# Attention placed from slot 0, masks behind ReLUs, values in one slot: a windowed attention interleaved with an MLP

## The chip, the cores and the metric

The kernel runs on one core of a Trainium2 chip. The metric is device time in microseconds (us) of one execution. A ratio is the mean time of one kernel's fast runs over that of the other's of the same rounds, so it is not quite the ratio of the medians that are quoted. Engines are called as in the profile: PE is the tensor engine (PEld its weight loads), DVE the vector engine, ACT the scalar engine, POOL the GpSimd engine, SP the sync engine, which here only issues DMAs.

## The reference, cut to what matters

```python
# q, k, v: (8 batches, 8 heads, 576, 64) float32
scores = scale * np.matmul(q, k.transpose(0, 1, 3, 2))
mask = (rel >= 0) & (rel < 64)                 # causal, window of 64
attn = softmax(np.where(mask, scores, -1e9))
x = np.matmul(attn, v)                         # reshaped to (8, 576, 512)
h = (x.transpose(0, 2, 1) @ U @ V)             # low rank: U (576, 32), V (32, 576)
u = x + h.transpose(0, 2, 1)
out = u + np.maximum(u @ w_ch1, 0) @ w_ch2     # 512 -> 2048 -> 512
```

## The kernel before

The 8 x 576 rows make 9 chunks of 512 rows for the MLP. While the MLP of chunk c runs, the attention of batch b = c + 1 is woven into it. A chunk has 32 slots: slots 0 to 15 each compute one 128-row piece of the first product (four 512-column matmuls into a PSUM tile `psA`, then a ReLU that empties it, on DVE or ACT), slots 16 to 31 compute four row tiles of the second product, four quarters each, into `psU`. Work of the attention is appended to a slot and is issued behind that slot's MLP matmuls. In the traces DVE takes up its work in the order of issue; what that costs, waits of 0.22 to 0.49 us for ACT, is seen below.

Scores (`SC`) go to PSUM, ACT takes the exponential, and DVE multiplies by the mask at once:

```python
# in SC(j), one pair of heads; SC8 does the last block of all heads
nc.scalar.activation(out=dst, in_=sc[:], func=ACT.Exp, scale=scale)
if not spare:
    nc.vector.tensor_tensor(out=dst, in0=dst, in1=maskA..., op=ALU.mult)
```

The values of one row tile (`PV(t)`) are small matmuls into a PSUM tile of 2 x 512 float32 (`xr`), followed by a reciprocal and a multiplication on DVE. The low-rank product (`UM`) has 5 row tiles and 4 column groups of 32 in the array; the fifth tile reuses group 0:

```python
for t in ts:                                   # t = 0 .. 4
    g = t % 4
    nc.tensor.matmul(hh["ps"][g * R : (g + 1) * R, :], ub[odd][:, t, :],
                     x[:, t, :, :].rearrange("p h d -> p (h d)"),
                     start=(t < 4), stop=(t > 0))
```

The placement of the attention in the slots of a steady chunk, and of batch 1 in chunk 0:

```python
DVE_RELU = (1, 2, 3, 5, 6, 7, 9, 11)           # these ReLUs on DVE, the others on ACT
PLACE = {"S": [1, 1, 1, 4, 4], "PV": [9, 9, 12, 12, 12],
         "TX": [8, 9, 10, 11, 12], "U": [15], "V": [17, 18, 19],
         "UT": [18, 18, 19, 19, 20]}
PLACE_1 = {"T": [9, 9, 10, 10, 11, 11, 12, 12], "S": [10, 11, 12, 13, 13],
           "PV": [15, 15, 16, 17, 18], "U": [20], "V": [21, 22, 23],
           "UT": [23, 24, 25, 26, 27], "TX": [20, 22, 24, 26, 28]}
...
if b > 1:                                      # value rows shifted by half a tile, on DVE
    slots[8 if b == 2 else 0].append(lambda: shift_v(b, nc.vector.tensor_copy, range(NFULL)))
```

`T` transposes keys and queries of batch 1 on PE; `TX` does so for the next batch by DMA (SP issues ten DMA transposes per batch); `UT` turns the finished rows `un` into the next MLP input `uTc`, by DMA from batch 3 on. The second weight `w2b` is loaded in four pieces early in chunk 0, between the loads of batches 1 and 2.

The softmax here doesn't subtract the row's maximum and nothing guards it: scores larger than these inputs give would overflow.

Of the kernel before, what the change touches and what calls it, by code (L numbers as in the profile page):

```python
# [9 lines left out]
ALU = mybir.AluOpType  # L10

BF16 = mybir.dt.bfloat16
FP32 = mybir.dt.float32
# [3 lines left out]
def kernel(  # L17
# [11 lines left out]
    nc = tc.nc  # L29
    B, H, S, D = q.shape  # L30
    DM = H * D
    R = moe_U.shape[1]
    F = moe_w_ch1.shape[1]
    P = nc.NUM_PARTITIONS
    W = 64
# [202 lines left out]
    def attention(b, spare=False):  # L238
# [96 lines left out]
        def SC(j):  # L335
            def f():
# [10 lines left out]
                if not spare:  # L347
                    nc.vector.tensor_tensor(  # L348
                        out=dst, in0=dst, in1=maskA.rearrange("p g n w -> p g (n w)"), op=ALU.mult
                    )  # L350
            return f

        def SC8():
# [18 lines left out]
            dst = ptl[:]  # L372
            if not spare:
                mk = maskA[:, :, 2:3, :].rearrange("p g n w -> p n g w").to_broadcast([P, HP, 2, W])
                nc.vector.tensor_tensor(out=dst, in0=dst, in1=mk, op=ALU.mult)

        def PV(t):
            def f():
# [4 lines left out]
                packed = b >= NXU and len(blks) == 1  # L383
                if packed:
                    one = ps_tp.tile([P, CH], FP32, name="one", tag="tp")
                else:
                    xr = ps_big.tile([P, 2, CH], FP32, name="xr", tag="big")
                for h in range(H):
                    for blk in blks:
                        r0 = ((blk + odd) % 2) * W  # L390
                        if blk == 0:
                            rhs = va[:, 0, h, :]
                        elif blk % 2 == 1:
                            rhs = va[:, blk // 2, h, :]
                        else:
                            rhs = vb[:, blk // 2 - 1, h, :]
                        cols = slice((h % 4) * VW, (h % 4 + 1) * VW)
                        if packed:
                            dst = one[(h // 4) * W : (h // 4 + 1) * W, cols]
                        else:  # L400
                            dst = xr[r0 : r0 + W, h // 4, cols]
                        nc.tensor.matmul(  # L402
                            dst,
                            pts[:, h // 2, h % 2, blk, :] if blk < NB - 1 else ptl[:, h // 2, h % 2, :],
                            rhs,
                            start=True,
                            stop=True,
                        )
                if packed:
                    xv = one[:, 0 : 4 * VW].rearrange("p (h e) -> p h e", e=VW)  # L410
                    rcp = wk_pool.tile([P, 2, 4, 1], FP32, name="rcp", tag="rcp")
                    nc.vector.reciprocal(out=rcp[:, 0], in_=xv[:, :, D:VW])
                    for a in range(2):
                        rs = slice(a * W, (a + 1) * W)
                        nc.vector.tensor_tensor(
                            out=x[lo:hi, t, 4 * a : 4 * a + 4, :],
                            in0=xv[rs, :, 0:D],
                            in1=rcp[rs, 0].to_broadcast([W, 4, D]),
                            op=ALU.mult,
                        )  # L420
                    return
# [9 lines left out]
            return f  # L431

# [3 lines left out]
        def UM(ts):  # L436
            def f():
# [5 lines left out]
                for t in ts:  # L443
                    g = t % 4
                    nc.tensor.matmul(  # L445
                        hh["ps"][g * R : (g + 1) * R, :],
                        ub[odd][:, t, :],
                        x[:, t, :, :].rearrange("p h d -> p (h d)"),
                        start=(t < 4),
                        stop=(t > 0),  # L450
                    )
# [112 lines left out]
        tiles = list(range(NT))  # L564
        if odd and b >= NXU:
            tiles = tiles[1:] + tiles[:1]
        pcs["PV"] = [PV(t) for t in tiles]
# [17 lines left out]
    DVE_RELU = (1, 2, 3, 5, 6, 7, 9, 11)  # L585

    DVE_RELU_0 = (8, 9, 11, 13, 15)

    def mlp(c):
# [3 lines left out]
        def ch1(i):  # L593
            def f():
# [10 lines left out]
                if i in (DVE_RELU if c > 0 else DVE_RELU_0):  # L605
                    nc.vector.tensor_relu(out=c1[i][:], in_=ps[:])  # L606
                else:
                    nc.scalar.activation(out=c1[i][:], in_=ps[:], func=ACT.Relu)  # L608
# [29 lines left out]
        "S": [1, 1, 1, 4, 4],  # L638
        "PV": [9, 9, 12, 12, 12],
        "TX": [8, 9, 10, 11, 12],  # L640
        "U": [15],
        "V": [17, 18, 19],
        "UT": [18, 18, 19, 19, 20],
# [3 lines left out]
        "T": [9, 9, 10, 10, 11, 11, 12, 12],  # L647
        "S": [10, 11, 12, 13, 13],
        "PV": [15, 15, 16, 17, 18],
        "U": [20],  # L650
        "V": [21, 22, 23],
        "UT": [23, 24, 25, 26, 27],
# [3 lines left out]
        "S": [8, 8, 11, 11, 13],  # L656
        "PV": [16, 16, 18, 18, 20],
        "TX": [12, 13, 14, 15, 16],
# [69 lines left out]
    for c in range(NCH):  # L728
# [10 lines left out]
        if b < B:  # L739
# [14 lines left out]
            if b > 1:  # L754
                slots[8 if b == 2 else 0].append(lambda: shift_v(b, nc.vector.tensor_copy, range(NFULL)))
            place(b, ("S", "PV"), where)
# [37 lines left out]
```

## Time and profile before

| | before |
|---|---|
| median of the runs | 327.12 us (326.85 to 327.33, 4 runs) |
| profiled span | 325.1 us |
| PE busy | 309.4 us, 95% |
| steady chunk (starts of the first `psA` matmuls) | 33.28 us |
| a chunk of the MLP alone (the last whole one) | 27.63 us |

The page of the kernel before: busy time, the busy tenths of PE and of the DMA engines in 40 equal slices, and the costliest group of instructions (name of the tile written and read, shapes, count, busy us, mean ns of one, idle us of the engine before it and what ended that idle time).

```profile
PE 309.4 (95%) x2806; PEld 149.9 (46%) x2831; DVE 169.7 (52%) x311; ACT 96.8 (30%) x152; POOL 104.1 (32%) x134
...
PE   7789899999999999899999999999999999999995
...
DMA  7999999999999999999999993355300330020011
...
L597 PE MATMUL psA<-uTc,w1b 128*128 128x512 bf16 x576 | 131.9, 379 | 4.6 <-DVE c L606 2.9
```

PE is what bounds the kernel (95% busy), but until slice 24 (about 195 us) the DMA engines are 90% or more busy as well, all but the first slice. The idle time before `psA` is small in sum, and it sits in a few places. In the order of time of PE, chunk 5 of the kernel before (start, duration, line, operation, count, and in brackets the idle time just before and what ended it):

```profile
204.79 0.47 PE L326 MATMUL sc<-qf,kf 64*64 64x128 bf16 x23
205.45 2.75 PE L597 MATMUL psA<-uTc,w1b 128*128 128x512 bf16 x12 [0.18 <-DVE c L606]
208.58 1.89 PE L597 MATMUL psA<-uTc,w1b 128*128 128x512 bf16 x8 [0.39 <-DVE c L606]
...
211.04 2.76 PE L597 MATMUL psA<-uTc,w1b 128*128 128x512 bf16 x12
```

The first line shows only the part of its group that reaches into the window asked for. And DVE at the same time:

```profile
203.18 0.69 DVE L348 TENSOR_TENSOR pts<-pts,maskA 128x1024 bf16<-128x1024 bf16 x1 [0.49 <-ACT pts L346]
204.10 0.69 DVE L348 TENSOR_TENSOR pts<-pts,maskA 128x1024 bf16<-128x1024 bf16 x1 [0.23 <-ACT pts L346]
204.71 1.28 DVE L606 TENSOR_SCALAR c<-psA 128x512 bf16<-128x512 f32 x2
206.32 0.69 DVE L348 TENSOR_TENSOR pts<-pts,maskA 128x1024 bf16<-128x1024 bf16 x1 [0.33 <-ACT pts L346]
207.24 0.69 DVE L348 TENSOR_TENSOR pts<-pts,maskA 128x1024 bf16<-128x1024 bf16 x1 [0.22 <-ACT pts L346]
207.84 1.88 DVE L606 TENSOR_SCALAR c<-psA 128x512 bf16<-128x512 f32 x3
```

DVE stands at a mask until ACT has finished the exponential, while ReLUs whose inputs are complete or about to be queue up behind it (runs of two from 204.71 and of three from 207.84). There are only three PSUM buffers for `psA`, so PE waits for the ReLU. The bracket counts idle time after the modelled end of a matmul; from start to start the loss is larger, because matmuls overlap: 512-column matmuls of a steady stream start 216 ns apart, and the two gaps here are 0.25 and 0.55 us longer than they would otherwise be.

The low-rank product in the kernel before, in the order of time of PE:

```profile
183.95 0.61 PE L445 MATMUL pshh<-xs,ub 128*32 128x512 bf16 x5
184.49 1.68 PE L619 MATMUL psU<-w2b,c 128*128 128x512 bf16 x6
```

Four of the five start 4 ns apart; the fifth, on group 0 again, starts 216 ns after them. And the places where PE waits for DMA in chunks 0 and 2:

```profile
35.06 0.45 PE L262 MATMUL tpw<-ident,qg 96*64 96x96 bf16 x12 [1.27 <-DMA qg<-in_q_dram]
...
46.95 1.04 PE L619 MATMUL psU<-w2b,c 128*128 128x512 bf16 x4
48.30 1.04 PE L619 MATMUL psU<-w2b,c 128*128 128x512 bf16 x4
...
132.82 1.47 PE L597 MATMUL psA<-uTc,w1b 128*128 128x512 bf16 x6 [1.26 <-DMA uTc<-un]
```

The `psU` matmuls at 46.95 and 48.30 us use the second and third piece of `w2b`, and do not wait: the value matmuls of batch 1 stand between them.

Some matmul records are missing from a trace: now and then two `psU` matmuls seem to start 432 ns apart, which is twice 216. Such gaps are not counted as waits here.

### The profile page before, as it was taken

What the parts mean: (1) busy time and instruction counts of PE and PEld (TensorE: products, weight loads), DVE (VectorE), ACT (ScalarE), POOL (GpSimd) and SP (SyncE); (2) the same over time, 40 slices, a digit from 0 to 9 for tenths busy, and PEclk for the clock granted to TensorE, in tenths of its full rate; (3) what the DMA queues carried; (4) which work ended last, traced back from release to release, by engine and by line L of the source; (5) the groups of instructions that cost most, each with busy time, mean ns of one, the idle gap of its engine ahead of it and who ended that gap; (6) DMA issues with size and microseconds to landing.
All of it is one profiled execution on the core that took longest, in us unless ns stands there. A gap on an engine that the chain in (4) does not pass through costs nothing.

```text
span 325.1 us, 6773 instructions
## 1 busy us (share of the span) xinstructions
PE 309.4 (95%) x2806; PEld 149.9 (46%) x2831; DVE 169.7 (52%) x311; ACT 96.8 (30%) x152; POOL 104.1 (32%) x134
## 2 busy tenths in 40 slices
PE   7789899999999999899999999999999999999995
PEld 6544454544454444344444444444444444444442
DVE  4364686265557752585458554855476525115211
ACT  3636541327026220343033402440154002201400
POOL 8692697545545744475430500000000000000000
PEclk9999999999999999999999999999999999999999
DMA  7999999999999999999999993355300330020011
GB/s 112 164 224 195 162 193 160 118 188 176 129 147 227 128 141 142 225 144 149 134 204 185 103 175 105 65 95 93 109 2 3 87 115 8 2 97 32 2 65 65
DMA packets 151871, 39.56 MB, mean 122 GB/s; under 512 B 140960, under 2 KB 146080, under 8 KB 151840
## 3 DMA queue, kind: packets, MB, share of 16 engines
q0 software_dynamic: 100096, 18.36, 82.4%
q1 hardware_dynamic: 51744, 20.77, 36.5%
q8 instruction: 22, 0.36, 0.5%
q14 instruction: 9, 0.07, 0.1%
HBM read 37.14 MB, written 9.44 MB: 143 GB/s over the span
## 4 chain that ended last, share of the span: by engine, by line
PE 73%; DMA 12%; DVE 4%; ACT 4%; POOL 2%; SPq 2%; issue 1%; POOLq 0%; ACTq 0%
PE psU L619 33%; PE psA L597 30%; DMA qg<-in_q_dram 5%; ACT pts L346 3%; PE xr L402 3%; DMA vA<-in_v_dram 3%; DMA uTc<-un 3%; PE sc L326 2%; DMA qf<-qn 2%; PE psv L519 2%; SPq L285 1%; DVE pts L348 1%; PE pshh L445 1%; DVE c L606 1%; DVE un L532 1%
## 5 line engine op out<-in xcount | busy, mean ns | idle before, releaser
L597 PE MATMUL psA<-uTc,w1b 128*128 128x512 bf16 x576 | 131.9, 379 | 4.6 <-DVE c L606 2.9
L619 PE MATMUL psU<-w2b,c 128*128 128x512 bf16 x556 | 130.4, 379 | 1.2 <-issue 0.2
L608 ACT ACTIVATE c<-psA 128x512 bf16<-128x512 f32 x75 | 44.7, 598 | 167.8 <-PE psA L597 167.8
L597 PEld LDWEIGHTS <-w1b 128*128 128x128 bf16 x576 | 54.2, 98 | 68.7 <-issue 4.1
L619 PEld LDWEIGHTS <-c 128*128 128x128 bf16 x576 | 54.9, 98 | 65.8 <-issue 3.0
L628 DVE TENSOR_TENSOR osb<-psU,un 128x512 f32<-128x512 f32 x36 | 24.8, 690 | 79.6 <-PE psU L619 79.6
L606 DVE TENSOR_SCALAR c<-psA 128x512 bf16<-128x512 f32 x69 | 46.0, 686 | 20.7 <-PE psA L597 20.0
L135 POOL DMA_DIRECT2D vA<-in_v_dram x32 | 28.5, 898 | 25.6 <-PE one L402 12.9
L532 DVE TENSOR_TENSOR un<-psv,xs 128x512 bf16<-128x512 f32 (+1 forms) x40 | 25.9, 684 | 20.6 <-PE psv L519 20.4
L126 POOL DMA_DIRECT2D kn<-in_k_dram x30 | 25.9, 864 | 26.1 <-DMA vA<-in_v_dram 14.2
L346 ACT ACTIVATE pts<-sc 128x1024 bf16<-128x1024 f32 x32 | 31.4, 1029 | 3.0 <-PE sc L326 2.4
L126 POOL DMA_DIRECT2D qn<-in_q_dram x30 | 25.3, 845 | 13.8 <-DMA vA<-in_v_dram 5.7
L425 DVE TENSOR_TENSOR xs<-xr,rcp 128x512 bf16<-128x512 f32 (+1 forms) x35 | 24.2, 691 | 1.2
L348 DVE TENSOR_TENSOR pts<-pts,maskA 128x1024 bf16<-128x1024 bf16 x28 | 19.4, 695 | 9.2 <-ACT pts L346 9.2
L402 PEld LDWEIGHTS <-pts 128*64 128x64 bf16 x512 | 10.7, 110 | 8.4 <-issue 4.0
L326 PEld LDWEIGHTS <-kf 64*64 64x64 bf16 x704 | 9.9, 107 | 8.4 <-issue 8.2
L326 PE MATMUL sc<-qf,kf 64*64 64x128 bf16 (+1 forms) x624 | 12.3, 212 | 1.4 <-issue 0.3
L402 PE MATMUL xr<-vA,pts 128*64 128x65 bf16 x296 | 12.2, 196 | 0.6 <-ACT pts L346 0.4
L519 PE MATMUL psv<-hh,vrep 128*128 128x512 bf16 x40 | 12.6, 379 | 0.0
L424 DVE RECIPROCAL rcp<-xr 128x8 f32<-128x8 f32 (+1 forms) x35 | 7.1, 202 | 8.9 <-PE xr L402 8.6
L402 PE MATMUL xr<-vB,pts 128*64 128x65 bf16 x192 | 9.5, 196 | 0.7 <-DVE rcp L424 0.6
L554 ACT COPY uTc<-tpu 128x512 bf16<-128x512 bf16 x9 | 5.3, 585 | 11.2 <-PE tpu L551 11.2
(89 smaller groups left out, 130.9 us busy)
## 6 DMA issues: line engine op xcount, KB each, us to landing
out_dram<-osb SPq DMA_DIRECT2D x36, 256.0 KB, 3.3
vA<-in_v_dram POOLq DMA_DIRECT2D x32, 128.0 KB, 10.5
kn<-in_k_dram POOLq DMA_DIRECT2D x24, 128.0 KB, 11.9
qn<-in_q_dram POOLq DMA_DIRECT2D x24, 128.0 KB, 12.6
w1b<-in_moe_w_ch_dram POOLq DMA_DIRECT2D x2, 1024.0 KB, 16.0
w2b<-in_moe_w_ch_dram POOLq DMA_DIRECT2D x4, 512.0 KB, 12.8
kg<-in_k_dram POOLq DMA_DIRECT2D x2, 288.0 KB, 5.6
qg<-in_q_dram POOLq DMA_DIRECT2D x2, 288.0 KB, 6.3
```

Source lines behind the costliest of these rows:

```text
L126: nc.gpsimd.dma_start(out=dst[0:rows, t, :, :], in_=src[b, :, t * P : t * P + rows, :].rearrange("h p d -> p h d"),)
L135: nc.gpsimd.dma_start(out=va[:, t, :, 0:D], in_=v[b, :, t * P : (t + 1) * P, :].rearrange("h p d -> p h d"),)
L326: nc.tensor.matmul(sc[g][r0 : r0 + W, col * W : (col + n) * W], keys_of(j, u, rs), queries_of(j, blk, n, rs), start=not spare, stop=last o ...
L346: nc.scalar.activation(out=dst, in_=sc[:], func=ACT.Exp, scale=scale)
L402: nc.tensor.matmul(dst, pts[:, h // 2, h % 2, blk, :] if blk < NB - 1 else ptl[:, h // 2, h % 2, :], rhs, start=True, stop=True,)
L425: nc.vector.tensor_tensor(out=x[lo:hi, t, :, :].rearrange("p (a h) d -> p a h d", a=2), in0=xv[:, :, :, 0:D], in1=rcp[lo:hi].to_broadcast( ...
L532: nc.vector.tensor_tensor(out=u_tiles[g][rs, :], in0=ps[0][rs, n, :], in1=x[rs, t, :, :].rearrange("p h d -> p (h d)"), op=ALU.add,)
L597: nc.tensor.matmul(ps[:], w1b[:, dc, i * P : (i + 1) * P], uTc[:, :, dc, :], start=(dc == 0), stop=(dc == NDC - 1),)
L606: nc.vector.tensor_relu(out=c1[i][:], in_=ps[:])
L608: nc.scalar.activation(out=c1[i][:], in_=ps[:], func=ACT.Relu)
L619: nc.tensor.matmul(acc[t][:], c1[i][:, t * P : (t + 1) * P], w2b[:, i, :], start=(i == 0), stop=(i == NFC - 1),)
L628: nc.vector.tensor_tensor(out=osb[:], in0=acc[t][:], in1=u_tiles[g][:], op=ALU.add)
```

## The change

Its intent: start the attention of a steady chunk one slot earlier; issue each mask after the next ReLUs instead of right after its exponential; do all values of a batch in one slot with fewer, wider evacuations; split the fifth tile of the low-rank product over the four column groups; shift the values of the next batch in slot 24 of the chunk before; and move batch 1's attention two slots back, away from a wait for its queries. (In chunk 1 the transposes for batch 3 also come one slot later, and the masks of batches 1 and 2 become pieces of their own.)

```diff
-                if not spare:
-                    nc.vector.tensor_tensor(... maskA ...)         # mask inside SC(j)
+        def MK(j):                                                 # mask as a piece of its own
+            def f():
+                nc.vector.tensor_tensor(out=dst, in0=dst, in1=maskA..., op=ALU.mult)
 ...
+        def PVA():                                                 # all values of a batch
+            wide = [ps_big.tile([P, 2, CH], FP32, ...) for _ in range(2)]   # heads 0 to 6
+            rest = psum["mm"].tile([P, CH], FP32, ...)                      # head 7
+            one = ps_tp.tile([P, CH], FP32, ...)                            # the half tile
+            ... 72 matmuls, then per tile one reciprocal and one multiplication ...
 ...
-                    g = t % 4
-                    nc.tensor.matmul(hh["ps"][g * R : (g + 1) * R, :], ..., start=(t < 4), ...)
+                    if t < 4:
+                        nc.tensor.matmul(hh["ps"][t * R : (t + 1) * R, :], ..., start=True, ...)
+                        continue
+                    for g in range(4):
+                        cols = slice(g * P, (g + 1) * P)
+                        nc.tensor.matmul(hh["ps"][g * R : (g + 1) * R, cols],
+                                         ub[odd][:, t, :], xt[:, cols], start=False, stop=True)
 ...
-        pcs["PV"] = [PV(t) for t in tiles]
+        pcs["PV"] = [PVA] if b >= NXU else [PV(t) for t in range(NT)]      # NXU = 3
 ...
-    DVE_RELU = (1, 2, 3, 5, 6, 7, 9, 11)
-    DVE_RELU_0 = (8, 9, 11, 13, 15)
+    DVE_RELU = {0: (8, 10, 11, 13, 15), 1: (2, 4, 6, 9, 10, 12, 13)}
+    DVE_RELU_N = (0, 1, 2, 4, 5, 6, 8)
 ...
     PLACE = {
-        "S": [1, 1, 1, 4, 4],  "PV": [9, 9, 12, 12, 12],  "TX": [8, 9, 10, 11, 12],
-        "U": [15],  "V": [17, 18, 19],  "UT": [18, 18, 19, 19, 20],
+        "S": [0, 0, 0, 3, 3],  "M": [0, 1, 2, 4, 5],  "PV": [8],  "TX": [6, 7, 8, 9, 10],
+        "U": [14],  "V": [16, 17, 18],  "UT": [17, 17, 18, 18, 19],
     }
     PLACE_1 = {
-        "T": [9, 9, 10, 10, 11, 11, 12, 12],  "S": [10, 11, 12, 13, 13],
-        "PV": [15, 15, 16, 17, 18],  "U": [20],  "V": [21, 22, 23],  "UT": [23, ..., 27],
+        "T": [11, 11, 12, 12, 13, 13, 14, 14],  "S": [12, 13, 14, 15, 15],
+        "M": [13, 14, 15, 16, 16],
+        "PV": [17, 17, 18, 19, 20],  "U": [22],  "V": [23, 24, 25],  "UT": [25, ..., 29],
     }
 ...                                                                # shift of values
-            if b > 1: slots[8 if b == 2 else 0].append(... shift_v(b) ...)
+            for bs, slot in ((b, 8), (b + 1, 24)):
+                if 1 < bs < B and (slot == 24) == (bs > 2): slots[slot].append(... shift_v(bs) ...)
```

More of the change, by code (lines that the diff above doesn't have):

```diff
@@ L346, in f, with MK8 @@
                 nc.scalar.activation(out=dst, in_=sc[:], func=ACT.Exp, scale=scale)
-                if not spare:
-                    nc.vector.tensor_tensor(
-                        out=dst, in0=dst, in1=maskA.rearrange("p g n w -> p g (n w)"), op=ALU.mult
-                    )
-            return f
+            return f
+        def MK(j):
+            def f():
+                dst = pts[:, j, :, :, :].rearrange("p g n w -> p g (n w)")
+                nc.vector.tensor_tensor(
+                    out=dst, in0=dst, in1=maskA.rearrange("p g n w -> p g (n w)"), op=ALU.mult
+                )
+            return f
+        def MK8():
+            mk = maskA[:, :, 2:3, :].rearrange("p g n w -> p n g w").to_broadcast([P, HP, 2, W])
+            nc.vector.tensor_tensor(out=ptl[:], in0=ptl[:], in1=mk, op=ALU.mult)
         def SC8():
@@ L371, in SC8, with values @@
                 nc.scalar.activation(out=ptl[:, :, ga:gb, :], in_=src, func=ACT.Exp, scale=scale)
-            dst = ptl[:]
-            if not spare:
-                mk = maskA[:, :, 2:3, :].rearrange("p g n w -> p n g w").to_broadcast([P, HP, 2, W])
-                nc.vector.tensor_tensor(out=dst, in0=dst, in1=mk, op=ALU.mult)
+        def values(dst, h, blk):
+            if blk == 0:
+                rhs = va[:, 0, h, :]
+            elif blk % 2 == 1:
+                rhs = va[:, blk // 2, h, :]
+            else:
+                rhs = vb[:, blk // 2 - 1, h, :]
+            nc.tensor.matmul(
+                dst,
+                pts[:, h // 2, h % 2, blk, :] if blk < NB - 1 else ptl[:, h // 2, h % 2, :],
+                rhs,
+                start=True,
+                stop=True,
+            )
         def PV(t):
@@ L381, in f @@
                 hi = W if (not odd and t == NT - 1) else P
-                packed = b >= NXU and len(blks) == 1
-                if packed:
-                    one = ps_tp.tile([P, CH], FP32, name="one", tag="tp")
-                else:
-                    xr = ps_big.tile([P, 2, CH], FP32, name="xr", tag="big")
+                xr = ps_big.tile([P, 2, CH], FP32, name="xr", tag="big")
                 for h in range(H):
@@ L390, in f @@
                         r0 = ((blk + odd) % 2) * W
-                        if blk == 0:
-                            rhs = va[:, 0, h, :]
-                        elif blk % 2 == 1:
-                            rhs = va[:, blk // 2, h, :]
-                        else:
-                            rhs = vb[:, blk // 2 - 1, h, :]
-                        cols = slice((h % 4) * VW, (h % 4 + 1) * VW)
-                        if packed:
-                            dst = one[(h // 4) * W : (h // 4 + 1) * W, cols]
-                        else:
-                            dst = xr[r0 : r0 + W, h // 4, cols]
-                        nc.tensor.matmul(
-                            dst,
-                            pts[:, h // 2, h % 2, blk, :] if blk < NB - 1 else ptl[:, h // 2, h % 2, :],
-                            rhs,
-                            start=True,
-                            stop=True,
-                        )
-                if packed:
-                    xv = one[:, 0 : 4 * VW].rearrange("p (h e) -> p h e", e=VW)
-                    rcp = wk_pool.tile([P, 2, 4, 1], FP32, name="rcp", tag="rcp")
-                    nc.vector.reciprocal(out=rcp[:, 0], in_=xv[:, :, D:VW])
-                    for a in range(2):
-                        rs = slice(a * W, (a + 1) * W)
-                        nc.vector.tensor_tensor(
-                            out=x[lo:hi, t, 4 * a : 4 * a + 4, :],
-                            in0=xv[rs, :, 0:D],
-                            in1=rcp[rs, 0].to_broadcast([W, 4, D]),
-                            op=ALU.mult,
-                        )
-                    return
+                        cols = slice((h % 4) * VW, (h % 4 + 1) * VW)
+                        values(xr[r0 : r0 + W, h // 4, cols], h, blk)
                 xv = xr[lo:hi, :, 0 : 4 * VW].rearrange("p a (h e) -> p a h e", e=VW)
@@ L431, in PV @@
             return f
+        def PVA():
+            t0 = 1 if odd else 0
+            ts = list(range(t0, t0 + NFULL))
+            single = 0 if odd else NT - 1
+            blk1 = 0 if odd else NB - 1
+            HB = H - 1
+            wide = [ps_big.tile([P, 2, CH], FP32, name="xw", tag="big") for _ in range(2)]
+            rest = psum["mm"].tile([P, CH], FP32, name="xe", tag="mm")
+            one = ps_tp.tile([P, CH], FP32, name="one", tag="tp")
+            for n in range(2):
+                for m, t in enumerate(ts[2 * n : 2 * n + 2]):
+                    for h in range(H):
+                        for r, blk in enumerate((2 * t - odd, 2 * t + 1 - odd)):
+                            rs = slice(r * W, (r + 1) * W)
+                            if h < HB:
+                                dst = wide[n][rs, m, h * VW : (h + 1) * VW]
+                            else:
+                                c = (2 * n + m) * VW
+                                dst = rest[rs, c : c + VW]
+                            values(dst, h, blk)
+            for h in range(4):
+                for a in range(2):
+                    values(one[a * W : (a + 1) * W, h * VW : (h + 1) * VW], 4 * a + h, blk1)
+            ev = rest[:, 0 : NFULL * VW].rearrange("p (t e) -> p t e", e=VW)
+            rce = wk_pool.tile([P, NFULL, 1], FP32, name="rce", tag="rce")
+            nc.vector.reciprocal(out=rce[:], in_=ev[:, :, D:VW])
+            nc.vector.tensor_tensor(
+                out=x[:, t0 : t0 + NFULL, HB, :],
+                in0=ev[:, :, 0:D],
+                in1=rce[:].to_broadcast([P, NFULL, D]),
+                op=ALU.mult,
+            )
+            for n in range(2):
+                xv = wide[n][:, :, 0 : HB * VW].rearrange("p m (h e) -> p m h e", e=VW)
+                rcp = wk_pool.tile([P, 2, HB, 1], FP32, name="rcw", tag="rcw")
+                nc.vector.reciprocal(out=rcp[:], in_=xv[:, :, :, D:VW])
+                nc.vector.tensor_tensor(
+                    out=x[:, ts[2 * n] : ts[2 * n] + 2, 0:HB, :],
+                    in0=xv[:, :, :, 0:D],
+                    in1=rcp[:].to_broadcast([P, 2, HB, D]),
+                    op=ALU.mult,
+                )
+            ov = one[:, 0 : 4 * VW].rearrange("p (h e) -> p h e", e=VW)
+            rco = wk_pool.tile([P, 4, 1], FP32, name="rco", tag="rco")
+            nc.vector.reciprocal(out=rco[:], in_=ov[:, :, D:VW])
+            xo = x[W:P] if odd else x[0:W]
+            for a in range(2):
+                rs = slice(a * W, (a + 1) * W)
+                nc.vector.tensor_tensor(
+                    out=xo[:, single, 4 * a : 4 * a + 4, :],
+                    in0=ov[rs, :, 0:D],
+                    in1=rco[rs].to_broadcast([W, 4, D]),
+                    op=ALU.mult,
+                )
@@ L443, in f @@
                 for t in ts:
-                    g = t % 4
-                    nc.tensor.matmul(
-                        hh["ps"][g * R : (g + 1) * R, :],
-                        ub[odd][:, t, :],
-                        x[:, t, :, :].rearrange("p h d -> p (h d)"),
-                        start=(t < 4),
-                        stop=(t > 0),
-                    )
+                    xt = x[:, t, :, :].rearrange("p h d -> p (h d)")
+                    if t < 4:
+                        nc.tensor.matmul(
+                            hh["ps"][t * R : (t + 1) * R, :], ub[odd][:, t, :], xt,
+                            start=True, stop=False,
+                        )
+                        continue
+                    for g in range(4):
+                        cols = slice(g * P, (g + 1) * P)
+                        nc.tensor.matmul(
+                            hh["ps"][g * R : (g + 1) * R, cols], ub[odd][:, t, :], xt[:, cols],
+                            start=False, stop=True,
+                        )
                 if ts[-1] == NT - 1:
@@ L563, in attention @@
         pcs["S"].insert(0 if b >= NXU else HP, SC8)
-        tiles = list(range(NT))
-        if odd and b >= NXU:
-            tiles = tiles[1:] + tiles[:1]
-        pcs["PV"] = [PV(t) for t in tiles]
+        if not spare:
+            pcs["M"] = [MK(j) for j in range(HP)]
+            pcs["M"].insert(0 if b >= NXU else HP, MK8)
+        pcs["PV"] = [PVA] if b >= NXU else [PV(t) for t in range(NT)]
         pcs["U"] = [UM((t,)) for t in range(NT)] if spare else [UM(tuple(range(NT)))]
@@ L604, in f @@
                 c1[i] = c1_pool.tile([P, CH], BF16, name=f"c1_{i}")
-                if i in (DVE_RELU if c > 0 else DVE_RELU_0):
+                if i in DVE_RELU.get(c, DVE_RELU_N):
                     nc.vector.tensor_relu(out=c1[i][:], in_=ps[:])
@@ L637 @@
     PLACE = {
-        "S": [1, 1, 1, 4, 4],
-        "PV": [9, 9, 12, 12, 12],
-        "TX": [8, 9, 10, 11, 12],
-        "U": [15],
-        "V": [17, 18, 19],
-        "UT": [18, 18, 19, 19, 20],
+        "S": [0, 0, 0, 3, 3],
+        "M": [0, 1, 2, 4, 5],
+        "PV": [8],
+        "TX": [6, 7, 8, 9, 10],
+        "U": [14],
+        "V": [16, 17, 18],
+        "UT": [17, 17, 18, 18, 19],
     }
@@ L646 @@
     PLACE_1 = {
-        "T": [9, 9, 10, 10, 11, 11, 12, 12],
-        "S": [10, 11, 12, 13, 13],
-        "PV": [15, 15, 16, 17, 18],
-        "U": [20],
-        "V": [21, 22, 23],
-        "UT": [23, 24, 25, 26, 27],
+        "T": [11, 11, 12, 12, 13, 13, 14, 14],
+        "S": [12, 13, 14, 15, 15],
+        "M": [13, 14, 15, 16, 16],
+        "PV": [17, 17, 18, 19, 20],
+        "U": [22],
+        "V": [23, 24, 25],
+        "UT": [25, 26, 27, 28, 29],
         "TX": [20, 22, 24, 26, 28],
@@ L656 @@
         "S": [8, 8, 11, 11, 13],
+        "M": [9, 10, 12, 13, 14],
         "PV": [16, 16, 18, 18, 20],
-        "TX": [12, 13, 14, 15, 16],
+        "TX": [13, 14, 15, 16, 17],
         "U": [21],
@@ L753 @@
                 slots[6].append(lambda: nc.scalar.copy(out=ub[1][:], in_=uf[1][:]))
-            if b > 1:
-                slots[8 if b == 2 else 0].append(lambda: shift_v(b, nc.vector.tensor_copy, range(NFULL)))
-            place(b, ("S", "PV"), where)
+            for bs, slot in ((b, 8), (b + 1, 24)):
+                if 1 < bs < B and (slot == 24) == (bs > 2):
+                    slots[slot].append(
+                        lambda bs=bs: shift_v(bs, nc.vector.tensor_copy, range(NFULL))
+                    )
+            place(b, ("S", "M", "PV"), where)
             if NXB <= b + 1 < B:
```

## The prediction

> **What bounds the kernel now.** The tensor engine: the page gives PE 95% busy of 325.1 us. In the order of time, 512-column matmuls of the two MLP products start every 216 ns, and a chunk of the MLP alone (the last whole one) takes 27.63 us. Chunks 0 to 4 start at 23.54, 63.72, 98.12, 132.82 and 166.11 us; the steady ones take 33.28 us, 5.65 of it attention and waits.
>
> **What the change takes from a steady chunk**:
> 1. ReLU waits. Before `psA` the engine waits for `DVE c` twice per chunk, 0.25 us after the second group of scores and 0.55 us a slot later, because DVE masks (0.69 us each) stand ahead of ReLUs in order. With masks behind ReLUs, my hand timeline of DVE (ReLU 0.6 to 0.69, mask 0.69, small mask 0.43) leaves no wait: -0.80 us.
> 2. One value slot instead of two. [...] 309 ns instead of 216 before a 128x64 group, 127 instead of 26 after it. One round trip less: about -0.2 us. The wide evacuations end (estimate, scaled from 0.69 us per 512 elements) 1 us before the low-rank matmul.
> 3. Low-rank tail. The fifth 512-column `pshh` matmul starts 216 ns after the other four, which start 4 ns apart. As four 128-column pieces in different column groups it should cost about 56 ns: -0.16 us per batch.
> Sum: about 32.1 us instead of 33.28.
>
> **Where the gain is lost.** DMA is 90% or more busy until about 185 us.
> - Chunk 0: the move by two slots removes the 1.45 us wait for `qg` (landing 35.0 us), but `w2b`'s four pieces land at 41.6, 44.2, 46.7 and 49.2 us. The values that filled that time before now come after it, so PE waits there (about 2.4 us); the fourth quarter starts at 49.3, and two value tiles (0.49 us each) follow. Chunk 1 starts near 64.1 instead of 63.7.
> - Chunk 1: the 0.44 us wait for `qf` vanishes, but the shift of batch 3's values now stands at slot 24, and their last load landed at 92.3 us; `un` waits behind it, a transpose perhaps 0.4 us. Chunk 2 starts near 98.3, as before.
> - Chunk 2: the 1.42 us wait for the transposed `uTc` (landing 132.8) stays about half: transposes of keys and queries start at the end of the scores, 0.7 us earlier, and the `uTc` ones precede an output store. Chunk 3 near 131.2, chunk 4 near 163.4.
> Then three chunks at -1.15 us.
>
> **Prediction.** 2.7 us gained at chunk 4's start, 3.4 after it: 6.1 us, so 327.17 becomes 321.1 us, range 319.6 to 323.0. Faster by over 2% (below 320.6) 0.33, within 2% 0.66, slower 0.01.
>
> **What would show it.** Idle time before `psA` from `DVE c` near 0; one `xw`/`xe`/`one` group per steady chunk; `pshh` to `psU` under 0.4 us; steady chunks of 32.1 us; new waits of `psU` for `DMA w2b` at 44 to 49 us; no 1.3 us wait of `tpw` for `qg`; a shorter `uTc` wait near 131 us.
>
> **What would make it wrong.** `w2b` or batch 3's values landing at other times; the wide evacuation delaying the low-rank matmul; ReLUs, now packed into slots 0 to 8 of DVE, waiting behind late masks; key and query transposes landing late for scores at slot 0.

The 0.2 us are (309 - 216) + (127 - 30) = 190 ns of the trace (the 26 of the text is nearer 30 there), and the sum is still 0.80 + 0.2 + 0.16 = 1.16 us off 33.28. The 56 ns of part 3 are an estimate; in the same trace the 128-column `tpu` transposes of a tile start 55 to 56 ns apart.

## The result, and the profile after

The changed kernel took 321.59 us in the median (320.92 to 322.46, 4 runs) against 327.12 us before: ratio 0.9833, 95% interval 0.9807 to 0.9858. The predicted 321.1 us (a ratio of 0.9815 to the 327.17 us then known) is 0.5 us off, and the time lies in the predicted range. Run again as a control (label `c1_after` below, in a call of its own) it had the ratio 0.9796, 0.9748 to 0.9843, which by the same rule is "unclear".

| start of chunk, us | 0 | 1 | 2 | 3 | 4 | 5 | 6 | 7 | 8 |
|---|---|---|---|---|---|---|---|---|---|
| before | 23.54 | 63.72 | 98.12 | 132.82 | 166.11 | 199.39 | 232.67 | 265.94 | 293.57 |
| predicted | | 64.1 | 98.3 | 131.2 | 163.4 | | | | |
| after | 23.69 | 64.51 | 98.31 | 131.66 | 163.76 | 195.86 | 227.95 | 260.04 | 287.67 |

The steady chunks 3 to 6 of the changed kernel take 32.10 us each. 2.35 us are won by the start of chunk 4, and 3.55 us in chunks 4 to 6. The same lines of the page after:

```profile
PE 304.6 (95%) x2829; PEld 148.9 (47%) x2855; DVE 163.1 (51%) x293; ACT 101.8 (32%) x160; POOL 103.2 (32%) x134
...
PE   6879988999999999899999999999999999999995
...
DMA  7999999999999999999999994444200520020011
...
L665 PE MATMUL psU<-w2b,c 128*128 128x512 bf16 x555 | 130.3, 379 | 3.6 <-DMA w2b<-in_moe_w_ch_dram 2.3
L643 PE MATMUL psA<-uTc,w1b 128*128 128x512 bf16 x576 | 131.0, 380 | 1.6 <-DMA uTc<-un 1.1
```

The idle time that `DVE c` ended before `psA` is gone, and a new wait of `psU` for `w2b` has come, as predicted. Chunk 5 of the changed kernel on PE, in the order of time:

```profile
196.96 0.63 PE L326 MATMUL sc<-qf,kf 64*64 64x64 bf16 x36
197.52 2.76 PE L643 MATMUL psA<-uTc,w1b 128*128 128x512 bf16 x12
200.21 0.65 PE L326 MATMUL sc<-qf,kf 64*64 64x128 bf16 x36
200.80 4.49 PE L643 MATMUL psA<-uTc,w1b 128*128 128x512 bf16 x20
...
206.51 5.35 PE L643 MATMUL psA<-uTc,w1b 128*128 128x512 bf16 x24
211.79 0.40 PE L487 MATMUL pshh<-xs,ub 128*32 128x512 bf16 x4
212.02 0.23 PE L495 MATMUL pshh<-xs,ub 128*32 128x128 bf16 x4
212.18 1.04 PE L643 MATMUL psA<-uTc,w1b 128*128 128x512 bf16 x4
```

No line has a bracket: PE waits for nothing in this chunk. The line left out is the one group of values. DVE in the same stretch:

```profile
198.59 0.69 DVE L652 TENSOR_SCALAR c<-psA 128x512 bf16<-128x512 f32 x1 [0.29 <-PE psA L643]
199.20 0.68 DVE L352 TENSOR_TENSOR pts<-pts,maskA 128x1024 bf16<-128x1024 bf16 x1
199.80 0.69 DVE L652 TENSOR_SCALAR c<-psA 128x512 bf16<-128x512 f32 x1
200.40 0.68 DVE L352 TENSOR_TENSOR pts<-pts,maskA 128x1024 bf16<-128x1024 bf16 x1
201.87 0.69 DVE L652 TENSOR_SCALAR c<-psA 128x512 bf16<-128x512 f32 x1 [0.79 <-PE psA L643]
202.48 0.68 DVE L352 TENSOR_TENSOR pts<-pts,maskA 128x1024 bf16<-128x1024 bf16 x1
```

Masks and ReLUs alternate, and none of these 0.69 us masks waits for ACT any more: in this stretch DVE's only idle time is waiting for PE, which is the right way round. Only the small mask of the last block, just before this stretch, still waits 0.26 us for ACT in each steady chunk; PE loses nothing by it. The waits for DMA in chunks 0 and 2 of the changed kernel:

```profile
35.51 0.42 PE L262 MATMUL tpw<-ident,qg 96*64 96x96 bf16 x12
...
44.57 1.02 PE L665 MATMUL psU<-w2b,c 128*128 128x512 bf16 x4 [0.33 <-DMA w2b<-in_moe_w_ch_dram]
...
47.09 1.02 PE L665 MATMUL psU<-w2b,c 128*128 128x512 bf16 x4 [0.86 <-DMA w2b<-in_moe_w_ch_dram]
49.63 1.02 PE L665 MATMUL psU<-w2b,c 128*128 128x512 bf16 x3 [1.13 <-DMA w2b<-in_moe_w_ch_dram]
...
131.66 1.04 PE L643 MATMUL psA<-uTc,w1b 128*128 128x512 bf16 x4 [1.09 <-DMA uTc<-un]
```

The wait for the queries `qg` is gone, and three waits for the pieces of `w2b` stand in its place: 0.49, 0.93 and 1.21 us from start to start beyond the usual distance. The transposed `uTc` still holds up chunk 3.

### The profile page after: what moved, and what is told of

The parts are those of the page before. It is cut to its first block, busy times and chain, and to the rows that moved or that the text cites. A ratio compares the mean times of both kernels' runs of the same rounds, so it can differ in the third digit from the quotient of the medians.

```text
span 319.2 us, 6811 instructions
## 1 busy us (share of the span) xinstructions
PE 304.6 (95%) x2829; PEld 148.9 (47%) x2855; DVE 163.1 (51%) x293; ACT 101.8 (32%) x160; POOL 103.2 (32%) x134
## 4 chain that ended last, share of the span: by engine, by line
PE 80%; DMA 13%; POOL 5%; issue 1%; DVE 0%; POOLq 0%
PE psU L665 36%; PE psA L643 35%; DMA qg<-in_q_dram 5%; DMA vA<-in_v_dram 3%; DMA uTc<-un 3%; PE psv L566 2%; DMA qn<-in_q_dram 2%; PE sc L326 2%; PE xw L388 2%; POOL vB L149 1%; POOL vB L152 1%; PE xr L388 1%; PE pshh L487 1%; PE tpu L598 1%; POOL kg L117 1%
## 5 line engine op out<-in xcount | busy, mean ns | idle before, releaser
L654 ACT ACTIVATE c<-psA 128x512 bf16<-128x512 f32 x83 | 49.6, 597 | 91.3 <-PE psA L643 91.2
L652 DVE TENSOR_SCALAR c<-psA 128x512 bf16<-128x512 f32 x61 | 42.1, 690 | 25.8 <-PE psA L643 25.8
L379 ACT ACTIVATE ptl<-low 128x256 bf16<-128x256 f32 x5 | 1.9, 384 | 65.8 <-PE high L326 65.8
L455 DVE TENSOR_TENSOR xs<-xw,rcw 128x896 bf16<-128x896 f32 x10 | 10.9, 1092 | 0.3
L411 DVE TENSOR_TENSOR xs<-xr,rcp 128x512 bf16<-128x512 f32 (+1 forms) x15 | 10.4, 690 | 0.5
L502 ACT CAST hh<-pshh 128x512 bf16<-128x512 f32 x7 | 4.1, 581 | 16.9 <-PE pshh L495 16.9
```

The costliest lines, as they stand in the source:

```text
L652: nc.vector.tensor_relu(out=c1[i][:], in_=ps[:])
L654: nc.scalar.activation(out=c1[i][:], in_=ps[:], func=ACT.Relu)
```

## The experiments

Theory: the gain comes from three independent parts of the steady chunks, and everything before chunk 4 is held by DMA landings, so what is saved there is mostly not passed on. Rivals: the start in slot 0 or the moved shift took the waits away, not the order of masks and ReLUs; PE binds everywhere, so every saved piece of PE time counts in all batches; the move of batch 1 paid for itself. Twelve kernels ran.

### The control

The changed kernel, unaltered.

> The changed kernel again, as the control of this call. Theory: the time saved comes from three parts of the steady chunks (ReLU waits 0.80 us, one tiling round trip 0.2 us, low-rank tail 0.16 us); before chunk 3 the time is set by DMA landings. So the steady chunks are again 32.1 us each, chunk 3 starts near 131.5 us with a wait of about 1 us for the transposed u tiles, and the time is 321 to 322 us.

321.91 us in the median, 319.46 to 323.33 in 4 runs. Chunks 4 to 6 took 32.09 to 32.10 us. But chunk 3 started at 132.49 us, after a start-to-start wait of 2.1 us beyond the usual, and chunk 3 itself took 33.65 us instead of 32.10. The windows view of this run for the first 3.4 us of that trouble (stretch, its length, busy us and count of each engine, then the granted clock of PE, the DMA share and GB/s):

```profile
133.00:136.40 3.40, 3.40 (x59) 1.66 (x58) 1.12 (x2) 2.11 (x4) 1.59 (x3) 0.50 1.38 263
```

The granted clock was 0.50 over this stretch (called a spell of half clock from here on), 0.95 over the whole of chunk 3, and 1.00 in chunks 2 and 4 of the same run. From the 0.95 (an estimate) the spell is 0.05 x 33.65 / 0.5 = 3.4 us long. What it costs is the difference of the chunk: 33.65 - 32.10 = 1.55 us. This was not in the prediction; it is followed up at the end of this section.

### Masks ahead of ReLUs again

```diff
-        "M": [0, 1, 2, 4, 5],
+        "M": [0, 0, 0, 3, 3],
```

> Masks back ahead of the ReLUs in the steady chunks (each mask right after its exponentials), nothing else. Theory: DVE works in order and stands at a mask until the exponentials are done while finished ReLU inputs hold the PSUM buffers; PE then waits about 0.2 us after the second group's scores and 0.5 to 0.6 us a slot later: steady chunks of about 32.9 us, 324 us in all. Rival: it is starting the scores in slot 0, or moving the value shift out of slot 0, that took the waits away; then the chunks stay at 32.1 us.

324.93 us (323.9 to 325.35). The steady chunks took 32.88 us, 0.78 us more than 32.10, and both waits came back where they had been:

```profile
203.91 2.75 PE L643 MATMUL psA<-uTc,w1b 128*128 128x512 bf16 x12 [0.19 <-DVE c L652]
207.05 0.81 PE L643 MATMUL psA<-uTc,w1b 128*128 128x512 bf16 x3 [0.39 <-DVE c L652]
```

Scores from slot 0, values in one slot and the moved shift are all still in this kernel, so the rival falls: it is the order on DVE.

### Values in two slots again

```diff
-        pcs["PV"] = [PVA] if b >= NXU else [PV(t) for t in range(NT)]
+        pcs["PV"] = [PV(t) for t in tiles]          # with the old evacuations
-        "PV": [8],
+        "PV": [8, 8, 11, 11, 11],
```

> Values again tile by tile in two slots (8 and 11) with the old evacuations, nothing else. Theory: one more round trip of the tiling mode per chunk, about 0.2 us: steady chunks of 32.3 us, about 0.8 us in all, no new wait on DVE. Rival: the wide evacuation is what matters (7 DVE instructions fewer per chunk); then the difference is a wait before the low-rank matmul or before psA, not in the gaps at the mode changes.

322.38 us (321.43 to 323.91). The steady chunks took 32.35 us, 0.25 us more, with no new wait of PE in them. So what one slot saves is a round trip of the tiling mode (`128*128` to `128*64` and back): 93 ns on the way in (309 instead of 216, start to start) and about 100 on the way out (127 instead of about 30) are 0.2 us of the 0.25; the rest is not accounted for. The wide evacuation, 1.09 us for 896 elements and off the critical path, is not what pays.

### The low-rank tail whole again

```diff
-                    for g in range(4):
-                        cols = slice(g * P, (g + 1) * P)
-                        nc.tensor.matmul(hh["ps"][g * R : (g + 1) * R, cols], ..., start=False, stop=True)
+                    g = t % 4
+                    nc.tensor.matmul(hh["ps"][g * R : (g + 1) * R, :], ..., start=(t < 4), stop=(t > 0))
```

> The low-rank tail whole again in all eight batches. Theory: 0.16 us per batch on PE, but only chunks 3 to 6 pass it on to the end, since chunk 0 is held by the landing of the second weight and chunk 2 by the u transposes: steady chunks 32.26 us, 0.5 to 0.7 us in all. Rival: PE binds throughout, so all eight batches count: 1.3 us.

322.85 us (321.55 to 324.36). The profile of this kernel in chunk 4, in the order of time of PE:

```profile
181.65 0.60 PE L486 MATMUL pshh<-xs,ub 128*32 128x512 bf16 x5
182.19 1.04 PE L637 MATMUL psA<-uTc,w1b 128*128 128x512 bf16 x4
```

From the first `pshh` to the next product it is 0.54 us, against 0.39 us (211.79 to 212.18) in the changed kernel: 0.15 us. The steady chunks took 32.25 us, which is the same 0.15. In this kernel's trace chunk 0 passed nothing on: chunk 1 started at 63.38 us, earlier than in the changed kernel, because `w2b` happened to land 1.3 us earlier (48.3 instead of 49.6 us). It also had a spell of half clock at the start of chunk 3, as the control had (granted clock 0.50 from 132.80 to 136.20 us). Whether 0.5 to 0.7 or 1.3 us were lost in all, the times cannot tell: the medians differ by 0.9 us from the control's, inside the spread of either kernel.

The three parts add up: 0.78 + 0.25 + 0.15 = 1.18 us, and the steady chunk went from 33.28 to 32.10, which is 1.18 us. By this sum nothing is left for the start in slot 0 (undone alone below) or for the moved shift (not undone alone) in a steady chunk.

### Batch 1 back in its old slots

```diff
-        "T": [11, 11, 12, 12, 13, 13, 14, 14],  "S": [12, 13, 14, 15, 15],  "M": [13, 14, 15, 16, 16],
-        "PV": [17, 17, 18, 19, 20],  "U": [22],  "V": [23, 24, 25],  "UT": [25, 26, 27, 28, 29],
+        "T": [9, 9, 10, 10, 11, 11, 12, 12],  "S": [10, 11, 12, 13, 13],  "M": [11, 12, 13, 14, 14],
+        "PV": [15, 15, 16, 17, 18],  "U": [20],  "V": [21, 22, 23],  "UT": [23, 24, 25, 26, 27],
-    DVE_RELU = {0: (8, 10, 11, 13, 15), ...
+    DVE_RELU = {0: (8, 9, 11, 13, 15), ...
```

> Batch 1's attention back to its old slots (with its old ReLU split and each mask one slot after its scores); the rest as changed. Theory: chunk 0 is bound by landings either way: the 1.4 us wait for the queries comes back, the 2.4 us for the second weight go to nearly nothing, and chunk 1 starts at 63.3 to 63.8 us instead of 64.5; what is won is used up by the waits for the landings in chunks 1 and 2, so the time is within 0.5 us of the changed kernel. Rival: the move by two slots paid for itself by removing the 1.4 us wait: this kernel is 1 us or more slower.

321.35 us (320.2 to 324.56), ratio 0.9822: not told from the changed kernel, but with this spread the times could not show the rival's 1 us either, so the trace has to decide. Chunk 1 started at 63.83 us, 0.7 us earlier than in the changed kernel, with no wait for `w2b`. By chunk 2 the lead had become a loss of 0.5 us (98.81 against 98.31): batch 2's scores in chunk 1 now waited 0.95 us for the landing of transposed queries. Chunk 3 started at 132.34 us. In the two traces of the changed kernel it started at 131.66 and 132.49 us. So the move by two slots shows no gain beyond the difference of those two; it exchanged one wait for DMA for another. The wait for `qg` was only 0.4 us in this run, as chunk 0 had started 1.3 us later; the granted clock of the profiled run was 0.992, against 0.999 in the changed kernel's first trace.

### The steady attention one slot later

```diff
-        "S": [0, 0, 0, 3, 3],  "M": [0, 1, 2, 4, 5],  "PV": [8],  "TX": [6, 7, 8, 9, 10], ...
+        "S": [1, 1, 1, 4, 4],  "M": [1, 2, 3, 5, 6],  "PV": [9],  "TX": [7, 8, 9, 10, 11], ...
-    DVE_RELU_N = (0, 1, 2, 4, 5, 6, 8)
+    DVE_RELU_N = (1, 2, 3, 5, 6, 7, 9)
```

> The steady chunks' attention one slot later throughout (scores from slot 1, ReLU list shifted by one). Theory: in the chunks that PE binds nothing changes (32.1 us); only the wait at the end of chunk 2 grows, as key and query transposes, and the u transposes behind them, are issued about 0.9 us later: chunk 3 starts 0.6 to 0.9 us later, 0.6 to 1.2 us in all. Rival: the start in slot 0 is worth something in every chunk; then steady chunks are longer than 32.1 us.

324.77 us (323.37 to 325.6), ratio 0.9897: about 3 us slower than the changed kernel, where 0.6 to 1.2 were expected. The chunks that PE binds took 32.09 to 32.10 us, so the rival falls and the start in slot 0 is worth nothing there. The loss lies where it was expected, but it is larger:

```profile
134.68 0.61 PE L643 MATMUL psA<-uTc,w1b 128*128 128x512 bf16 x1 [3.01 <-DMA uTc<-un]
```

Chunk 3 waited 3.2 us instead of 1.3 us and started 3.0 us later; 1.1 us of that is the late start of chunk 2, which the spell in chunk 0 named below had caused. Then came a spell of half clock in chunk 3 (33.68 us, 1.58 us more). A first spell had already come in chunk 0, behind the waits for `w2b`, and chunk 1 had started at 65.62 us. The windows view of this run:

```profile
49.20:52.60 3.40, 3.35 (x23) 1.34 (x23) 1.42 (x3) 0.00 (x0) 2.52 (x4) 0.50 2.43 155
134.50:137.90 3.40, 3.22 (x8) 1.04 (x8) 0.00 (x0) 0.60 (x1) 1.02 (x2) 0.50 1.46 237
```

All four runs of this kernel had a granted clock between 0.987 and 0.992. One spell costs 0.5 x 3.4 / 322 = 0.005 of it, so (an estimate) about two spells in three of the runs and at least one in the fourth. The expectation left that term out.

### Fewer loads (wrong results on purpose)

```diff
-            if b + 1 < B: load_v(b + 1)
-            if b + 2 < B: load_kq(b + 2, False)
+            if b + 1 < 5: load_v(b + 1)
+            if b + 2 < 5: load_kq(b + 2, False)
+            elif b + 2 < B: loaded[b + 2] = (kn[b % 2], qn[b % 2])     # what lies there
```

> Wrong results on purpose: batches 5 to 7 load no queries, keys and values and use those that lie there, so that the DMA engines have less to do from about 105 us on. Theory: the 1.2 us wait for the u transposes at the end of chunk 2 comes from the loaded DMA engines (8.3 us from issue to landing); without the loads it falls to 2.5 to 5 us and the wait goes: chunk 3 starts at about 130.4 us, 1.2 us less in all. Rival: the issue of the transposes on their queue (1.3 to 1.6 us each, ten ahead of them) sets it; then the wait stays above 0.8 us.

Wrong results; 321.12 us (319.71 to 321.68). Chunk 3 started at 130.44 us, with no wait for `uTc`. The time from issue to landing of the five `uTc` transposes of that chunk, in the changed kernel:

```profile
DMA to landing us min/median/max: 7.5/8.3/8.5
```

and without the later loads:

```profile
DMA to landing us min/median/max: 2.4/2.5/4.3
```

The transposes were issued only 1.2 us earlier than in the changed kernel (from 118.98 instead of 120.23 us) and landed 6.5 us earlier (the third one at 125.1 instead of 131.6 us). It is the load on the DMA engines that sets the landing, not the issue. The time as a whole did not show the 1.2 us clearly: the profiled run had a granted clock of 0.989, against 0.999 in the changed kernel's first trace, which over 318.0 us is (an estimate) 3.2 us of full clock less.

### One u tile transposed by PE

```diff
-                if b >= NXU:
+                if b >= NXU and (b, t) != (NXU, 2):
                     nc.sync.dma_start_transpose(out=dst, in_=u_tiles[g][:])
                     return
+    PLACE_3 = dict(PLACE, UT=[17, 17, 21, 18, 19])          # batch 3
```

> The third u tile of batch 3, the one whose landing chunk 3 waits for, is transposed by PE (0.22 us) in slot 21 instead of by DMA; nothing else. Theory: the tile before it landed at 130.0 us, so chunk 3 starts at about 130.6 us instead of 131.7; nothing later takes that back, and the time falls by about 1.0 us. Rival: the next DMA landing takes the place of this one, in chunk 3 or at its end; then less than 0.4 us is left.

320.52 us (320.27 to 321.84), ratio 0.9789. The wait ahead of chunk 3 was 0.4 us, now for the tile before (landing 132.4 us). Chunk 2 took 32.71 us, against 33.35 and 34.24 us in the two traces of the changed kernel. In this run PE was slow at 49.75 us, where four `psU` matmuls took 1.86 us instead of the 1.02 us at 47.20 (granted clock of the run 0.993); chunk 1 started only at 66.03 us, and the run ended all the same at a span of 320.1 us. PE reached this wait 1.5 us later, and the tile before landed 2.4 us later, than in the changed kernel's first trace, so how much of the shorter wait is due to the edit this trace does not show; nor do the times, whose interval (0.9738 to 0.9841) holds both ratios of the changed kernel. Chunks 3 to 6 took 32.10 us each, so nothing later took time back.

### Batch 1's values packed ahead of the landing

```diff
-        "PV": [17, 17, 18, 19, 20],
+        "PV": [17, 17, 18, 18, 18],
```

> Batch 1's last two value tiles moved from slots 19 and 20 to slot 18, ahead of the fourth quarter of the second weight; nothing else. Theory: their 0.5 us each fall into the wait for that landing, so chunk 1 starts about 1 us earlier (63.5 us instead of 64.5); about 0.3 us of it is left at the end, as the key and query landings and the u transposes of chunks 1 and 2 take the rest. Rival: PE binds, and the whole 1 us is left.

322.45 us (321.87 to 324.02), ratio 0.9859. Chunk 1 started at 63.53 us, 1.0 us earlier, as expected. Nothing of it was left: the profile of this kernel in chunk 1, in the order of time of PE, shows where it went.

```profile
71.39 0.36 PE L326 MATMUL sc<-qf,kf 64*64 64x128 bf16 x12
72.92 0.50 PE L326 MATMUL sc<-qf,kf 64*64 64x128 bf16 x24 [1.17 <-DMA qf<-qn]
```

The scores of batch 2 came 1 us earlier to a landing that was not earlier (72.88 us, against 71.73 in the changed kernel's trace, where they did not wait), and chunk 2 started at 98.71 us, chunk 3 at 132.94. The rival, that PE binds and the whole 1 us stays, falls.

### Three waits taken away together

The packing above, two `uTc` tiles of batch 3 by PE, and batch 3's last-block scores in slot 3:

```diff
+                if b >= NXU and not (b == NXU and t in (1, 2)):
+    PLACE_3 = dict(PLACE, UT=[17, 20, 21, 18, 19], S=[3, 0, 0, 3, 3], M=[5, 1, 2, 4, 5])
+        "PV": [17, 17, 18, 18, 18],                          # batch 1
```

> The previous kernel's packing, two u tiles of batch 3 (third and second) transposed by PE, and batch 3's last-block scores in slot 3 instead of 0. Theory: no wait of more than 0.4 us is left at the start of chunks 2 and 3; chunk 3 starts at about 130.3 us instead of 131.7 to 132.5, the steady chunks are the same 32.1 us, and the time is about 1.5 us below the changed kernel (near 319.5 to 320 us). With no long wait of PE left, the half clock seen after waits of 2 us and more does not come at 49 or 133 us. Rival: the landings just move the wait to the end of chunk 3; then at most 0.5 us is won.

320.52 us (320.13 to 321.51), ratio 0.9797. Chunk 2 took 32.54 us, which is 32.10 and two PE transposes of 0.22 us, with no wait; chunk 3 started at 130.99 us. The first part of the expectation failed: chunk 1 still lost 0.9 us to the queries and 0.6 us to the shift of batch 3's values, and the time is above the 319.5 to 320 us expected. The granted clock was 0.999 or more in all four runs; one spell takes about 0.005 off it (the estimate above), so (an estimate too) none of them had one.

### Batch 2's values in one slot

```diff
-        "S": [8, 8, 11, 11, 13],  "PV": [16, 16, 18, 18, 20],
+        "S": [8, 8, 11, 11, 11],  "PV": [16],                # batch 2, one slot, as from batch 3 on
```

> As the previous one, and batch 2 gets the one-slot values too, and its last-block scores join the second pair's slot: three round trips of the tiling mode fewer in chunk 1. Theory: about 0.6 us less in chunk 1 (33.2 us instead of 33.8), of which at least half is left at the end. Rival: chunk 1 is bound by landings, and nothing is left.

320.54 us (319.84 to 320.9, 5 runs), ratio 0.9794, 0.9769 to 0.9818. The edit stands on top of the previous version's. Chunk 1 took 34.48 us instead of 35.33 us. Without the waits (1.27 us here, 1.51 us there) that is 33.2 instead of 33.8 us, the 0.6 us expected; the rest is shorter waits. Chunk 3 started at 130.50 instead of 130.99 us. The times do not tell it from the version before. Both are the best versions found: about 1 us below the medians of the changed kernel (321.59 and 321.91 us), which those runs do not settle beyond doubt.

### Zeros in the waits

```diff
+                if c == 0 and t == 0 and quarter > 0:        # psU, before the real matmuls
+                    for _ in range((0, 1, 3, 4)[quarter]):
+                        nc.tensor.matmul(acc[t][:], idle[:, 0:P], idle[:], start=False, stop=False)
+                if c == 3 and i == 0:                        # psA
+                    for _ in range(5):
+                        nc.tensor.matmul(ps[:], idle[:, 0:P], idle[:], start=True, stop=True)
```

> The changed kernel with matmuls of zeros where PE waits: 1, 3 and 4 before the second to fourth quarter of the second weight in chunk 0, 5 before chunk 3 (216 ns each; sums unchanged). Theory: the spells of 3.4 us at half clock near 49 and 133 us, seen in three traces after long waits and costing about 1.6 us each, follow from PE standing idle; with the waits filled the landings and the starts of the chunks stay where they are in a trace without such a spell (64.5, 98.3, 131.7 us), none comes at 49 or 133 us, and times spread less than the 319.5 to 323.3 us of the changed kernel. Rival: the spells come at random; then they come here too.

322.29 us (321.13 to 323.09, 5 runs). In the profiled run the landings set the pace as before (chunks 1 to 3 at 64.18, 97.98 and 131.58 us), and the granted clock was 1.00 from 49 to 53 us and from 131 to 135 us: no spell there. But over the whole execution the five runs were granted 0.989 to 1.000 (the profiled one 0.995), so some of them ran below full clock somewhere; where, is not shown (in the profiled one not in these two stretches). So the clocks of this run decide nothing, and filling a wait with zeros did not make the kernel faster.

What the traces say of the spells together. At the start of chunk 3, the idle time of PE that `DMA uTc<-un` ended, and the clock granted right behind it:

| run | idle before `psA`, us | stretch, us | granted clock |
|---|---|---|---|
| `after` | 1.09 | 131.00 to 135.00 | 1.00 |
| `e8_batch1_values_packed` | 1.98 | 132.90 to 136.30 | 1.00 |
| `c1_after` | 1.99 | 133.00 to 136.40 | 0.50 |
| `e3_tail_whole` | 2.17 | 132.80 to 136.20 | 0.50 |
| `e5_slot_1` | 3.01 | 134.50 to 137.90 | 0.50 |

It is the same with the second and third wait for `w2b` in chunk 0. Behind 0.86 and 1.13 us of idle time in the changed kernel the clock stayed at 1.00 (47 to 51 us); behind 0.85 and 1.15 us in the run with one tile on PE four `psU` matmuls took 1.86 us instead of 1.02. So the length of a wait alone does not decide whether a spell follows: 1.98 us had none and 1.99 us had one. What decides it was not shown; that PE standing idle is the cause was the theory, and the run with zeros does not settle it. And a granted clock without a trace does not say where a spell lay: the nine runs of the last two tuned versions have 0.997 or more and four of the eight runs of the changed kernel 0.993 to 0.995, but 7 of the 23 runs of the kernel before have 0.987 to 0.995 as well.

## Why the prediction was right

- Steady chunks. Predicted 32.1 us, measured 32.10. Each of the three terms was confirmed by undoing it alone: ReLU waits 0.80 predicted and 0.78 measured, the mode change 0.2 and 0.25, the low-rank tail 0.16 and 0.15.
- The worry that ReLUs packed into the first slots of DVE would wait behind late masks did not come true: no PE wait is left in chunks 4 to 6.
- Chunk 0. The prediction said that the move by two slots would exchange the wait for the queries for about 2.4 us of waits for `w2b`, and chunk 1 would start at 64.1. Measured: waits of 0.49 + 0.93 + 1.21 = 2.6 us, and 64.51 us. `w2b`'s pieces landed 0.4 us later than in the trace before (the fourth at 49.59 instead of 49.21 us), which is the rest. The run with the old slots shows no gain of the move as such.
- Chunk 1. Predicted start of chunk 2: 98.3 us; measured 98.31. One of its terms, 0.4 us of waiting for `un` behind the shifted values, was not there in this run, as the values landed at 90.9 us instead of 92.3. It was there in four experiments (0.6 to 0.9 us). That 98.3 was met so closely is therefore luck: the 0.4 us by which chunk 1 started late and the 0.4 us of this wait cancel.
- Chunk 2. This is the term that was mis-sized. The wait for `uTc` was predicted to stay "about half" of 1.42 us; it was 1.26 us in the first trace of the changed kernel and 2.1 us in the control. The landing is set by the load on the DMA engines (8.3 us against 2.5 us without the loads), and it came 1.2 us earlier than before (131.61 instead of 132.77 us) where the predicted start of chunk 3 implied 1.6 us, while PE came 1.0 us earlier. That is 0.5 us in the first trace, about the whole error of the predicted time: 2.35 us were won by chunk 4 instead of 2.7, and 3.55 us after it instead of 3.4.
- Not foreseen at all: the spell of half clock behind the wait for `uTc` in the control (granted clock 0.50 over 3.40 us, behind 1.99 us of idle time), which cost a further 1.55 us. It did not happen in the profiled run of the result. In a time that is predicted from a trace without it, it is a risk on the slow side.

## What to carry to other kernels

Where an engine works in the order of issue, as DVE did here (0.78 us a chunk), issue first what can run now: a mask that still waits for another engine must not stand ahead of a ReLU whose input is complete, if that ReLU frees a buffer that the bounding engine needs. Before a stage is tuned, ask whether it is held by landings: then moving work inside it exchanges one wait for another, and pieces saved there are not passed on, while the same pieces count fully in the stages behind. And look at the granted clock behind long waits of the tensor engine: here stretches of 3.40 us at 0.50 followed idle times of 1.99, 2.17 and 3.01 us at the start of chunk 3, and cost 1.55 and 1.58 us in two of these runs, while 1.98 us in another run had no such stretch behind it. What decides it was not shown.
